# A long one-core attention, MLP and expert kernel: three pieces of the first batch are written at other places of its order

## The chip, the cores and the metric

The kernel runs on 1 core of a Trainium2 chip. Its time is the device time of one execution in microseconds (us); lower is better. Two times stand side by side below: the time of a run, and the span of one profiled execution, from its first to its last instruction. Engines are named as in the profile: PE is TensorE (matmul; PEld its weight loads), DVE is VectorE, ACT is ScalarE, POOL is GpSimd, SP is SyncE, which issues nearly all DMAs here.

## The reference: what is computed

The sizes are small enough to state: 4 batches, 12 heads, 448 positions, head dimension 64; a hard-swish MLP of 768 to 2048 to 768 on the 1792 tokens; then 8 experts of 768 to 1024 to 768, 224 tokens each.

```python
q_n, k_n = rmsnorm(q, g_q), rmsnorm(k, g_k)            # over the head dimension
scores = q_n @ k_n.T / 8
attn = exp(scores - max(scores)); attn /= sum(attn) + 1e-9
x = (attn @ v).transpose(0, 2, 1, 3).reshape(1792, 768)

h = x @ w_in                                           # w_in, w_out arrive in 64 bits
g = h * clip(h + 3, 0, 6) / 6
x2 = g @ w_out

logits = x2 @ w_gate          # greedy: the highest logits first, 224 tokens for each expert
out[tokens of e] = relu(x2[tokens of e] @ w1[e]) @ w2[e]
```

## The kernel before

**Tiling.** Attention works on pairs of heads: pair i (numbered from 0 in the code and in this text) holds two heads of one batch, so a batch is 6 pairs and there are 24. The first MLP matmul of batch b runs while the pairs of batch b+1 are worked on. A float32 product is split in a high and a low part (kh and kl, xh and xl, the two halves of w) and summed from three matmuls.

**The order is written out by hand.** In the part that the change touches, nothing is scheduled by a tool: every piece of work is put on a list with a number, its time in steps (`at(t, fn, ...)`), the list is sorted by that number, and each of the five engines then runs its own instructions in exactly that order. A pair starts every 16 steps. The steps are no clock, only places in the order; engines wait for one another by semaphores, and an instruction that waits holds all that stands behind it on its engine. SP is such a queue too: a DMA whose data is not there yet holds the DMAs behind it.

**What a pair needs, by name.** `squares` (ACT, L251) squares q and k of a pair; `fold` (POOL, L256) and `sums` (DVE, L267) add them up; `guess` (DVE, L271 and L272) makes a first inverse root and `invert` (POOL, L279 to L282, three rounds) refines it: the Newton steps. From pair 4 on two pairs share these small tiles and go through `guess` and `invert` together. `norm` (POOL, L298) scales q and k to `xn`; `transp` transposes them on PE (L315) and makes qh and kh on ACT (L324) and ql and kl on DVE (L327). `s1` makes scores on PE (L338) and their maxima mx on DVE (L341); `mt` transposes the maxima (PE L347) and lays them out as mr (DVE L349). `sT` makes the scores the other way round (PE L360) and ACT takes the exponent to ph (L371). `pv` multiplies by v (PE L449, copied out by ACT L452 to xn_t), `padd` and `psums` add the exponents up (POOL L442, PE L460 or L465, copied to rb by ACT L467).

**The trip of the sums.** The row sums leave for DRAM and come back in another shape: sum_dr (SP L471), rs (L476), reciprocal rr on DVE (L482, L483), rec_dr (L487), rb (L493, two DMAs). Then POOL multiplies (`xmul`, L497), ACT makes xh (L507) and POOL the low part xl (L505). The numbers `TX0` are the steps of these eight pieces for the pairs of the first batch.

**Narrowing.** w_in arrives in 64 bits. `conv` makes 32 bits of it in 16 units: a load of 768 KB (wraw, SP L159, 14 steps ahead), four steps (ACT L141, DVE L142, L143, L144, one step apart), and a store to DRAM (SP L174, one step behind the last). Two wraw buffers and two result buffers rotate. Unit u stands at `T_CI + D_CI * u`. From step 98 on the MLP of batch 0 loads the narrowed weights back (win_v, L181) and splits them (L118, L119).

PSUM is one pool of 8 banks that all matmuls take in turn, so a late reader of one bank can hold a later matmul.

Of the kernel before, what the change touches and what calls it, by code (L numbers as in the profile page):

```python
# [21 lines left out]
def kernel(  # L22
# [48 lines left out]
    T_SUMS, T_INV, T_INV0, NG0 = -50, -42, -35.5, 10  # L71
# [4 lines left out]
    T_ADD, T_PV, T_SUM = (6, 13), (15.6, 15.62, 15.64, 15.66), 15.7  # L76
    T_RS, T_RL, T_REC, T_RO, T_RB, T_X, T_XH, T_XL = 19.5, 21.5, 24, 25.5, 28, 33, 35.5, 39.5
    GD, WD2, C_ST = 12, 8, 5
    TX0 = (20, 23, 27, 29, 32.5, 39, 42, 46)
    QMAJOR = (NP - 1, B * NP - 1)  # L80
    T_CI, D_CI, T_CO, D_CO, T_CL = 20, 10, 180, 12, 14


    order = ExitStack()
# [652 lines left out]
    def at(t, fn, *args):  # L737
        events.append((t, len(events), fn, args))
# [7 lines left out]
    for i in range(NH // 2):  # L746
        t = 16 * i
        at(t + T_LOAD, load, i)
        at(t + T_VLOAD, vload, i)
        g = GROUP[i]  # L750
        first = 16 * g[0]
        t_sq = first + T_SUMS + 4 * (i - g[0])
        at(t_sq, squares, i)
        if 2 <= i < NG0:
            at(t_sq + 2, fold, i)
            t_sq += 3
        at(t_sq, sums, i)
        late_g = 4 <= g[0] < NG0
        if i == g[-1]:
            at(t_sq if 2 <= i < NG0 else first + T_INV, guess, g)  # L760
            at(first + (T_INV0 if late_g else T_INV), invert, g)
        at(t + (T_INV0 + 0.1 if late_g and i == g[0] else T_NORM), norm, i)
        at(t + T_Q, transp, i, 0)
        at(t + T_K, transp, i, 1)
        at(t + T_V, vsplit, i)
        for c in range(NCH):
            at(t + (T_S1[c] if i else -24 + 0.1 * c), s1, i, c)
            at(t + (T_ST[c] if i else (-9, -8.9, 1, 1.1)[c]), sT, i, c)
            if i in QMAJOR:
                for s in range(2):  # L770
                    at(t + T_AV[s][c], av, i, s, c)
            else:
                at(t + T_PV[c], pv, i, c)
        at(t + (T_MT if i else -21), mt, i)
        if i in QMAJOR:
            at(t + T_NUM, normalize, i)
            at(t + T_XT, xt, i)
        else:
            for n in range(2 if i >= NP else 0):
                at(t + T_ADD[n], padd, i, n)  # L780
            at(t + T_SUM, psums, i)
            tx = TX0 if i < NP else (T_RS, T_RL, T_REC, T_RO, T_RB, T_X, T_XH, T_XL)
            for d, fn in zip(tx, (rs_out, rs_in, rec, r_out, r_in, xmul)):
                at(t + d, fn, i)
            at(t + tx[6], xsplit, i, False)
            at(t + tx[7], xsplit, i, True)
        if (i + 1) % NP == 0:
            at(t + T_MLP[i // NP], mlp_next, i // NP)
# [1 line left out]
    at(8 * H + 2, prefetch, 0)  # L790
    at(8 * H + 14, prefetch)
    for u in range(NF if wide else 0):
        for out_, t in ((0, T_CI + D_CI * u), (1, T_CO + D_CO * u)):
            at(t - T_CL, conv, (out_, u), -1)
            for part in (0, 1, 2, 3, C_ST):
                at(t + part, conv, (out_, u), part)
# [446 lines left out]
    for pi, (t, hfs) in enumerate(passes):  # L1243
# [10 lines left out]
        for f in range(NF):  # L1254
            i, k = divmod(f, QF)
# [139 lines left out]
```

## Time and profile before

| | us |
|---|---|
| runs (3) | 1159.02, 1164.75, 1165.14; median 1164.75 |
| time of the profiled execution | 1162.06 |
| its span | 1160.2 |
| PE busy in it | 1099.2 (95%) |
| DVE, ACT, POOL busy | 692.2, 521.3, 464.6 |

The span is 1.9 us shorter than the time of the same execution, the part outside the first and last instruction. PE is busy nearly throughout from about 130 us on; its gaps lie in the first batch. A timeline row tells start, length, engine, line, operation and shapes, and in brackets how long the engine stood idle before it and what ended that. A row of the windows tells a stretch, its length, the busy time of each engine with its instruction count, the granted clock of TensorE as a share of full speed (1.00 is 2.4 GHz, 0.50 is 1.2 GHz, and values between are mixtures of the two), and the busy share and rate of the DMA engines.

### The profile page before, as it was taken

To read this page: it belongs to the slowest core of one execution; us is meant where nothing else is said; L and a number is where in the kernel's file an instruction comes from. 1 tells how busy PE (TensorE), PEld (TensorE's weight loads), DVE (VectorE), ACT (ScalarE), POOL (GpSimd) and SP (SyncE) were. 2 spreads that over 40 slices of the span, in tenths; PEclk is the share of its full clock that TensorE was granted. 3 is DMA by queue.
4 is the path that set the end of the run, shared out by engine and by line. 5 is a ranking of instruction groups with operands and counts; after the bars stand their busy time and mean duration, and the time that the engine had idled before them with its cause. 6 is when DMAs were issued, how large, how long until landed. Compare 5 with 4: busy or idle time off the path is not lost.

```text
span 1160.2 us, 19232 instructions
## 1 busy us (share of the span) xinstructions
PE 1099.2 (95%) x7073; PEld 880.7 (76%) x7073; DVE 692.2 (60%) x1440; ACT 521.3 (45%) x941; POOL 464.6 (40%) x410
## 2 busy tenths in 40 slices
PE   4978899999999999999999999999997999999997
PEld 3446556766766667787767888888887899999997
DVE  7877877886677845212341666666665846555550
ACT  4655555745545556533542111111114766666551
POOL 4665555664445533112444000000004677775540
PEclk9987989999999999999999999999998999999999
DMA  4575998978777887659996222222237888877731
GB/s 133 145 197 148 248 300 252 309 238 297 251 250 253 257 288 239 222 190 276 356 310 204 78 69 82 64 76 71 70 104 185 245 262 247 248 227 217 226 130 39
DMA packets 215357, 232.17 MB, mean 200 GB/s; under 512 B 28296, under 2 KB 188384, under 8 KB 215264
## 3 DMA queue, kind: packets, MB, share of 16 engines
q1 hardware_dynamic: 211936, 219.94, 61.6%
q0 software_dynamic: 3328, 11.01, 3.1%
q8 instruction: 55, 0.90, 0.3%
q14 instruction: 38, 0.31, 0.1%
HBM read 179.82 MB, written 51.09 MB: 199 GB/s over the span
## 4 chain that ended last, share of the span: by engine, by line
PE 67%; DVE 10%; DMA 9%; issue 5%; POOL 4%; ACT 3%; SPq 1%; POOLq 0%; DVEq 0%; ACTq 0%
PE y L1195 19%; PE h L559 15%; PE y L1347 8%; PE h L1283 5%; PE st L360 4%; PE av L449 4%; PE h L1285 3%; DMA w_hl<-w 2%; DMA we_s<-in_moe_w_dram 2%; DVE mx L341 2%; PE rt L988 1%; PE lg L601 1%; PE sm L465 1%; DMA gr<-g_dr 1%; DVE cv L143 1%
## 5 line engine op out<-in xcount | busy, mean ns | idle before, releaser
L559 PE MATMUL h<-xh,w 128*128 128x448 f32 x768 | 239.9, 382 | 1.0 <-DVE mx L341 0.5
L559 PEld LDWEIGHTS h<-xh,w 128*128 128x128 f32 x768 | 143.3, 191 | 35.9 <-issue 22.1
L559 PE MATMUL h<-xl,w 128*128 128x448 f32 x384 | 145.7, 379 | 0.0
L341 DVE TENSOR_REDUCE mx<-s 112x1 f32<-112x448 f32 x192 | 105.9, 611 | 51.6 <-PE s L338 51.3
L1133 ACT ACTIVATE g2h<-gr 128x512 fp32r<-128x512 f32 x60 | 37.9, 631 | 206.1 <-PE y L1195 161.6
L1195 PE MATMUL y<-woh,g2l 128*128 128x512 f32 (+1 forms) x448 | 124.8, 344 | 1.0 <-POOL g2l L1098 1.0
L1195 PE MATMUL y<-woh,g2h 128*128 128x512 f32 (+1 forms) x448 | 125.3, 345 | 0.0
L1195 PE MATMUL y<-wol,g2h 128*128 128x512 f32 (+1 forms) x448 | 125.2, 344 | 0.0
L1098 POOL TENSOR_TENSOR g2l<-gr,g2h 128x512 fp32r<-128x512 f32 x14 | 19.0, 1361 | 240.6 <-DMA gr<-g_dr 209.0
L119 POOL TENSOR_TENSOR wel<-we_s,weh 128x768 fp32r<-128x768 f32 x48 | 96.3, 2010 | 45.4 <-ACT weh L118 37.0
L118 ACT ACTIVATE weh<-we_s 128x768 fp32r<-128x768 f32 x107 | 88.4, 841 | 57.9 <-DMA we_s<-in_moe_w_dram 39.3
L119 DVE TENSOR_TENSOR wel<-we_s,weh 128x768 fp32r<-128x768 f32 x59 | 78.3, 1334 | 60.3 <-ACT weh L118 53.6
L371 ACT ACTIVATE ph<-st 112x448 f32<-112x448 f32 x192 | 93.0, 545 | 40.8 <-PE st L360 39.7
L442 POOL TENSOR_TENSOR pa<-ph 112x448 f32<-112x448 f32 x68 | 85.6, 1279 | 44.2 <-ACT ph L371 44.2
L1283 PE MATMUL h<-xe,weh 128*128 128x448 f32 x318 | 100.4, 375 | 2.0 <-DVE xe L1234 2.0
L559 PEld LDWEIGHTS h<-xl,w 128*128 128x128 f32 x384 | 73.2, 191 | 11.9 <-issue 7.0
L1195 PEld LDWEIGHTS y<-woh,g2l 128*128 128x128 f32 x448 | 72.0, 189 | 10.7 <-POOL g2l L1098 1.3
L1195 PEld LDWEIGHTS y<-woh,g2h 128*128 128x128 f32 x448 | 71.9, 189 | 10.6 <-issue 1.5
L1195 PEld LDWEIGHTS y<-wol,g2h 128*128 128x128 f32 x448 | 71.9, 189 | 9.1 <-issue 0.7
L1285 PE MATMUL h<-xe,wel 128*128 128x224 f32 x318 | 76.6, 268 | 0.0
L562 ACT ACTIVATE r<-h,half 128x448 f32<-128x448 f32 x64 | 40.6, 634 | 77.7 <-PE h L559 67.3
L497 POOL TENSOR_TENSOR xn_t<-xn_t,rb 128x448 f32<-128x448 f32 x22 | 25.8, 1175 | 119.7 <-DMA rb<-rec_dr 119.7
(252 smaller groups left out, 2386.1 us busy)
## 6 DMA issues: line engine op xcount, KB each, us to landing
we_s<-in_moe_w_dram SPq DMA_DIRECT2D x128, 384.0 KB
w<-w_hl SPq DMA_DIRECT2D x32, 768.0 KB
gr<-g_dr SPq DMA_DIRECT2D x52, 256.0 KB
wraw<-in_moe_w_in_dram SPq DMA_DIRECT2D x16, 768.0 KB
win_v<-w SPq DMA_DIRECT2D x32, 384.0 KB
w_hl<-w SPq DMA_DIRECT2D x16, 768.0 KB
wraw<-in_moe_w_out_dram SPq DMA_DIRECT2D x16, 768.0 KB
g_dr<-g SPq DMA_DIRECT2D x48, 224.0 KB
```

What stands on the lines that cost most here:

```text
L118: nc.scalar.activation(hi, raw, AF.Copy)
L119: eng.tensor_tensor(lo, raw, hi.bitcast(F32), op=OP.subtract)
L341: mx = nc.vector.tensor_reduce(MX[i][:, s, c:c + 1], pp[s][:CP, :S], axis=AX.X, op=OP.max)
L360: nc.tensor.matmul(pp[s][:CP, :S], a[r], b[r], start=(n == 0), stop=(n == len(todo) - 1))
L371: nc.scalar.activation(e, pp[s][:CP, :S], AF.Exp)
L442: nc.gpsimd.tensor_tensor(PA[i, s, n], PP[i, s, 2 * n][0], PP[i, s, 2 * n + 1][0], op=OP.add)
L449: nc.tensor.matmul(p[r, :S], vvs[i % 2][:, s, c, V0:V0 + 64], PP[i, s, c][0], start=(c == 0), stop=(c == NCH - 1))
L559: nc.tensor.matmul(p[:, :S], lhs[:, c], x[:, c], start=(n == 0), stop=(n == 3 * NC - 1))
L1195: nc.tensor.matmul(pp[hf][:, :COLS[hf].stop - COLS[hf].start], a[:, f % QF], w[:, COLS[hf]], start=(f == 0 and n == 0), stop=(f == NF - 1 ...
L1283: mm = [lambda: nc.tensor.matmul(p[:, :4 * CP], wh[:, fo], x.rearrange("d k t -> d (k t)"), start=(c == 0), stop=(c == NC - 1), skip_group ...
L1285: lambda: nc.tensor.matmul(p[:, :2 * CP], wl[:, fo], x[:, 0], start=False, stop=False, skip_group_check=True)]
L1347: nc.tensor.matmul(p[:CP, :HW], a[:, f, tk], w[:, o], start=(f == 0 and n == 0), stop=(f == FB - 1 and n == 2))
```

## The change

Three things move; no instruction is added or removed.

- For the pair groups (4, 5), (6, 7) and (8, 9) the second pair's squares, with its fold and sums, stand 2.1 steps later (6.1 instead of 4 steps behind the first). These second pairs are 5, 7 and 9 counted from 0.
- The narrowing units of w_in get a list of steps of their own: units 0 and 8 go 4.3 steps later, 3 and 11 go 6.3 later, 5 and 13 go 2.3 later, 6 and 14 go 1.7 earlier; the others stay. Loads and stores of a unit move with it.
- The low part xl of a first-batch pair stands at step 44.4 instead of 46.

```diff
-    TX0 = (20, 23, 27, 29, 32.5, 39, 42, 46)
+    TX0 = (20, 23, 27, 29, 32.5, 39, 42, 44.4)
...
-    T_CI, D_CI, T_CO, D_CO, T_CL = 20, 10, 180, 12, 14
+    T_CO, D_CO, T_CL = 180, 12, 14
+    T_CI = (24.3, 30, 40, 56.3, 60, 72.3, 78.3, 90, 104.3, 110, 120, 136.3, 140, 152.3, 158.3, 170)
...
-        t_sq = first + T_SUMS + 4 * (i - g[0])
+        late_g = 4 <= g[0] < NG0
+        t_sq = first + T_SUMS + (6.1 if late_g else 4) * (i - g[0])
...
-        for out_, t in ((0, T_CI + D_CI * u), (1, T_CO + D_CO * u)):
+        for out_, t in ((0, T_CI[u]), (1, T_CO + D_CO * u)):
```

PE's order is the same before and after. The new code is one line longer, so lines from 82 on count one higher in the rows of the change.

**The second squares and the narrowing of unit 3, on ACT.** These are ACT's instructions from pair 5's qh on; sq are the squares of pair 7, cv is the narrowing. Before:

```order
L324 ACTIVATE qh<-t,gq_72 128x448
L251 ACTIVATE sq<-ld_q 112x512
L251 ACTIVATE sq<-ld_k 112x512
L141 ACTIVATE cv<-wraw 128x768
L324 ACTIVATE kh<-t,gk 128x448
L304 ACTIVATE vv_134<-ld_v 112x8x64
L371 ACTIVATE ph<-st 112x448 x4
```

The same stretch in the changed kernel:

```order
L325 ACTIVATE qh<-t,gq_72 128x448
L325 ACTIVATE kh<-t,gk 128x448
L252 ACTIVATE sq<-ld_q 112x512
L252 ACTIVATE sq<-ld_k 112x512
L305 ACTIVATE vv_134<-ld_v 112x8x64
L372 ACTIVATE ph<-st 112x448 x4
L142 ACTIVATE cv<-wraw 128x768
```

kh moved ahead of three instructions; the narrowing step went behind the four exponents.

**The same place on DVE.** ql, kl and mr are the operands that PE waits for, st_2 the sums of the pair's squares, mx the maxima. Before:

```order
L327 SCALAR_TENSOR_TENSOR ql<-t,gq_72,qh 128x448
L142 TENSOR_SCALAR cv<-cv 128x768
L327 SCALAR_TENSOR_TENSOR kl<-t,gk,kh 128x448
L143 SCALAR_TENSOR_TENSOR cv<-wraw,cv 128x768
L267 TENSOR_REDUCE st_2_883<-sq 112x8 x2
L271 TENSOR_SCALAR st_2_883<-st_2_883 112x32
L272 TENSOR_SCALAR st_2_884<-st_2_883 112x32
L144 SCALAR_TENSOR_TENSOR cv<-wraw,cv 128x768
L349 TENSOR_TENSOR mr<-t,place 128x448
L341 TENSOR_REDUCE mx_130<-s_948 112x1
```

In the changed kernel:

```order
L328 SCALAR_TENSOR_TENSOR ql<-t,gq_72,qh 128x448
L328 SCALAR_TENSOR_TENSOR kl<-t,gk,kh 128x448
L350 TENSOR_TENSOR mr<-t,place 128x448
L268 TENSOR_REDUCE st_2_883<-sq 112x8 x2
L272 TENSOR_SCALAR st_2_883<-st_2_883 112x32
L273 TENSOR_SCALAR st_2_884<-st_2_883 112x32
L342 TENSOR_REDUCE mx_130<-s_942 112x1
L342 TENSOR_REDUCE mx_130<-s_943 112x1
L342 TENSOR_REDUCE mx_130<-s_966 112x1
L342 TENSOR_REDUCE mx_130<-s_967 112x1
L143 TENSOR_SCALAR cv<-cv 128x768
L144 SCALAR_TENSOR_TENSOR cv<-wraw,cv 128x768
```

kl and mr follow ql directly, and the narrowing steps (cv) went behind the four maxima, so ahead of rr.

**The trip of pair 4's sums on SP.** These are SP's DMAs from the sums' store on; w_97<-cv is the store of a narrowed unit, wraw the load of one. Before:

```order
L471 DMA sum_dr_1261<-rb 4x448
L236 DMA ld_v<-in_v_dram 112x2x256
L174 DMA w_97<-cv 128x6x128
L159 DMA wraw<-in_moe_w_in_dram 128x6x256
L476 DMA rs<-sum_dr_1261 112x2x8
L229 DMA ld_q<-in_q_dram 112x2x256
L229 DMA ld_k<-in_k_dram 112x2x256
L487 DMA rec_dr_1359<-rr 112x8
```

In the changed kernel:

```order
L472 DMA sum_dr_1258<-rb 4x448
L237 DMA ld_v<-in_v_dram 112x2x256
L477 DMA rs<-sum_dr_1258 112x2x8
L230 DMA ld_q<-in_q_dram 112x2x256
L230 DMA ld_k<-in_k_dram 112x2x256
L160 DMA wraw<-in_moe_w_in_dram 128x6x256
L488 DMA rec_dr_1360<-rr 112x8
```

The store and the load of a narrowing unit no longer stand between sum_dr and rs. On POOL the xl of pairs 1 and 3 moved from behind Newton steps and two xn ahead of those Newton steps, and the xl of pair 4 ahead of two pa.

## Rows read from the trace of the kernel before

**Rows 1.** Windows by stage: stretch, length, engines' busy time, clock, DMA share, GB/s.

```profile
38.00:65.00 27.00, 22.88 (x166) 11.94 (x166) 23.87 (x43) 17.93 (x35) 14.97 (x22) 1.00 0.58 156
65.00:83.00 18.00, 13.77 (x81) 6.62 (x77) 12.16 (x24) 8.50 (x17) 11.60 (x19) 0.81 0.71 198
96.00:116.00 20.00, 16.81 (x97) 13.86 (x95) 15.63 (x25) 9.18 (x17) 11.78 (x20) 0.70 0.49 130
130.00:170.00 40.00, 36.55 (x204) 26.91 (x205) 32.67 (x55) 21.95 (x40) 20.23 (x15) 0.90 0.88 262
400.00:1160.00 760.00, 739.44 (x4948) 641.72 (x4948) 387.72 (x892) 299.89 (x539) 252.97 (x172) 0.99 0.59 182
```

**Rows 2.** Timeline of PE: rows with a wait in front of them.

```profile
39.56 0.46 PE L338 MATMUL s<-kh,qh 64*112 64x448 f32 x2 [0.72 <-ACT kh L324]
...
51.19 0.32 PE L347 MATMUL t<-ident,mx 112*128 112x112 f32 x1 [1.28 <-DVE mx L341]
...
64.42 0.32 PE L347 MATMUL t<-ident,mx 112*128 112x112 f32 x1 [1.69 <-DVE mx L341]
...
67.23 0.71 PE L338 MATMUL s<-kh,qh 64*112 64x448 f32 x2 [1.50 <-ACT kh L324]
...
81.00 0.97 PE L338 MATMUL s<-kh,qh 64*112 64x448 f32 x2 [2.59 <-ACT xn_t L452]
...
97.58 0.46 PE L338 MATMUL s<-kh,qh 64*112 64x448 f32 x2 [1.00 <-ACT kh L324]
...
102.36 0.46 PE L360 MATMUL st<-mr,minus 64*112 64x448 f32 x2 [1.33 <-DVE mr L349]
...
162.82 0.71 PE L360 MATMUL st<-qh,kh 64*112 64x448 f32 x1 [2.68 <-DVE g L564]
```

**Rows 3.** Timeline of PE: the same 16 matmuls twice, and three marks without wait.

```profile
53.84 3.23 PE L449 MATMUL av<-ph,vv 112*64 112x448 f32 x16
...
69.75 5.01 PE L449 MATMUL av<-ph,vv 112*64 112x448 f32 x16
...
82.90 0.26 PE L347 MATMUL t<-ident,mx 112*128 112x112 f32 x1
...
115.43 0.39 PE L347 MATMUL t<-ident,mx 112*128 112x112 f32 x1
...
129.79 0.71 PE L360 MATMUL st<-qh,kh 64*112 64x448 f32 x2
```

**Rows 4.** Timeline of ACT ahead of pair 5's kh.

```profile
65.78 0.88 ACT L141 ACTIVATE cv<-wraw 128x768 f32<-128x768 f32 x1
66.56 0.62 ACT L324 ACTIVATE kh<-t,gk 128x448 fp32r<-128x448 f32 x1
```

**Rows 5.** Timeline of POOL and ACT around pair 1's low part.

```profile
69.93 1.77 POOL L497 TENSOR_TENSOR xn_t<-xn_t,rb 128x448 f32<-128x448 f32 x1 [3.10 <-DMA rb<-rec_dr]
...
71.74 0.58 ACT L507 ACTIVATE xh<-xn_t 128x448 fp32r<-128x448 f32 x1 [1.28 <-POOL xn_t L497]
...
79.25 1.13 POOL L505 TENSOR_TENSOR xl<-xn_t,xh 128x448 fp32r<-128x448 f32 x1
...
80.41 0.54 ACT L452 ACTIVATE xn_t<-av 128x448 f32<-128x448 f32 x1 [7.31 <-POOL xl L505]
```

**Rows 6.** The chain that ended last: start, length, what.

```profile
46.63 4.51 DMA rec_dr<-rr
...
64.23 5.57 DMA rb<-rec_dr
...
100.61 7.88 DMA rs<-sum_dr
```

**Rows 7.** Timeline of DVE: pair 4's row sums.

```profile
108.59 0.28 DVE L482 TENSOR_TENSOR rr<-rs 112x8 f32<-112x8 f32 x1 [4.16 <-DMA rs<-sum_dr]
```

**Rows 8.** Tile wraw, 30 to 130 us: one narrowing step, lengths in ns (min/median/max).

```profile
L143 DVE SCALAR_TENSOR_TENSOR cv<-wraw,cv x9: 947/962/2680, 41.8 to 117.1; 128x768 int32<-128x768 int32 x9
```

**Rows 9.** Timeline of POOL: pair 4's multiplication.

```profile
121.77 1.13 POOL L497 TENSOR_TENSOR xn_t<-xn_t,rb 128x448 f32<-128x448 f32 x1 [10.43 <-DMA rb<-rec_dr]
```

More of the change, by code (lines that the diff above doesn't have):

```diff
@@ L757 @@
         at(t_sq, sums, i)
-        late_g = 4 <= g[0] < NG0
         if i == g[-1]:
```

## The prediction

> **What bounds the kernel now.** I read the windows first. From 400 us on PE is busy 739 of 760 us at a clock of 0.99 [rows 1]: nothing in the change touches that part, and a microsecond won ahead of it stays won, because PE runs the same instructions in the same order and has no slack in which a late start could be caught up. So the question is only how much earlier PE comes out of the first batch. There the picture differs from window to window. From 38 to 65 us the clock is full and DVE is busy 23.87 of 27 us, PE 22.88: both are close to their limit. From 65 to 83 us, from 96 to 116 us and from 130 to 170 us no engine is that full, and the clock is granted at 0.81, 0.70 and 0.90 [rows 1], which means that for a part of these stretches TensorE ran at 1.2 instead of 2.4 GHz. What this costs is seen in a pair of rows: the same sixteen matmuls took 3.23 us at full clock and 5.01 us in a stretch with the lower one [rows 3]. Over a stretch the loss is its length times what the clock lacks: 18 x 0.19 = 3.4 us, 20 x 0.30 = 6.0 us, 40 x 0.10 = 4.0 us.
>
> Then I went down PE's timeline for the waits. Eight of them carry the argument [rows 2]: three for kh (0.72, 1.50 and 1.00), two for the last maxima (1.28 and 1.69), one for the copy xn_t on ACT (2.59), one for mr (1.33) and one at 162.82 for the MLP's g on DVE (2.68). Each of the three stretches with a lowered clock has one or several of these waits at its start or shortly before it.
>
> Last the engines behind those waits. ACT made the kh of pair 5 at 66.56, directly behind a narrowing step that began at 65.78 [rows 4], and in the order the two squares stand ahead of that. ACT's xn_t copy at 80.41 had stood idle 7.31 us for POOL's xl [rows 5], and POOL did that xl at 79.25, behind the Newton steps and both xn. DVE stood 4.16 us before rr [rows 7], for an rs that was 7.88 us under way [rows 6].
>
> **The change part by part.** I give for each stretch what could come back at most, and what I take.
>
> *38 to 65 us.* kh of pair 3 follows qh directly, so the wait of 0.72 goes. Ahead of the four maxima one long narrowing step (0.96 us, the median of L143 [rows 8]) goes behind them, so the maxima and the matmul that waits for them (1.28, later 1.69) come earlier. But DVE has only 3.1 us of slack in these 27 and its work stays the same, so what moves behind these maxima stands ahead of the next ones. At most 0.72 + 1.28 + 1.69 = 3.7 us come back, at least 0.7; I take 0.7 + half of 2.97 = **2.2 us**, which puts the mark at 64.42 at about 62.2.
>
> *65 to 83 us.* The 1.50 us wait for kh goes, as ACT no longer has squares and narrowing in front of it. The 2.59 us wait for xn_t goes too, since xl is done before the Newton steps. With the PE gaps gone the clock may stay up: 3.4 us. Together 7.5 us at most. Something else becomes late, though: the Newton steps now wait for xh and xl. Counted from the end of xn_t (69.93 + 1.77 = 71.70), the Newton steps and two xn took until 79.25, where xl began: 7.5 us [rows 5]. With xh (0.58) and xl (1.13) in front all this ends 1.7 us later, counted from the landing of rb, and PE needs those xn for the transposes ahead of its mark at 82.90 [rows 3]. So the wait for xn_t is in part replaced by one for xn. I take half of 7.5 less 1.7 = **2.0 us**; bounds: a loss of 1.7 and a gain of 7.5.
>
> *83 to 116 us.* kh (1.00) and mr (1.33) are no longer late: kl and mr follow ql on DVE with no narrowing between. With the clock's 6.0 us that is 8.3 us at most. Also rs now leaves ahead of the unit's store and its 768 KB load, not behind them; if it then takes about the 4.51 us of the rec_dr in [rows 6], which had such a load in front of it, DVE's 4.16 us wait shrinks by 3.4 us. That wait has narrowing and the maxima for the mark at 115.43 behind it, so it is what makes the rest usable and is not counted a second time. Against it stands the second xl ahead of Newton steps, 1.7 us. Half of 8.3 less 1.7 gives **2.4 us**; bounds: a loss of 1.7 and a gain of 8.3. The mark at 115.43 would then be near 109.
>
> *116 to 130 us.* Here the change costs. Unit 8's narrowing moves behind the last maxima, so one long step (0.96) more stands ahead of the reciprocal of pair 5, and POOL does an xl (1.13) before the two pa that PE waits for: **2.1 us** later, nothing if the earlier rb gives POOL its room, 3.0 us if both long steps count.
>
> *130 to 170 us.* Unit 11's narrowing leaves the place between ql, kl and g. The wait of 2.68 goes, and the lowered clock behind it (4.0 us) may: 6.7 us at most. But the DMA engines are busy 0.88 of this stretch [rows 1], and the split weights come when they land. I take half, **3.3 us**; bounds 0 and 6.7.
>
> The later units 5, 6, 13 and 14 I cost at nothing: what hides them is the distance in the order, since each unit's store still stands several loads ahead of the one that reads it back. If that cover were gone, the MLP would wait for unit 13 by its 2.3 steps, about 2.3 us (the 32 steps of two pairs take from 82.90 to 115.43 [rows 3], 1.0 us a step).
>
> Sum: 2.2 + 2.0 + 2.4 - 2.1 + 3.3 = 7.8 us. The profiled execution took 1162.06 us (span 1160.2); this gives 1154.3. The profiled execution lies 2.7 us under the median of the runs, and the four times together have a mean of 1162.7, so I name **1155 us**.
>
> A rule of the Trainium skill speaks against the new places of the narrowing. L143 takes 0.96 us as a rule, and 2.68 us in the longest of nine cases [rows 8]. The Trainium skill, page "SBUF — State Buffer", section "Who interferes with whom", says that DVE and GpSimd share a pair of ports as an exclusive lock: a DVE instruction with two inputs in SBUF contends with a GpSimd instruction that reads SBUF, and the one that comes second is blocked. By that rule the maxima, which come from PSUM, never suffer, and every narrowing step that is moved beside POOL's Newton steps can; the trace has such a long case, but the row alone doesn't show what stood in its way. The second rival below is worked out from the row, without the rule.
>
> **The rivals.**
>
> *All of it comes back.* If the clock stays up in all three stretches and no new wait comes, the halves that I took become wholes: 3.7 + 5.8 + 6.6 - 2.1 + 6.7 = 20.7 us. For it speaks that waits stand before each lowered stretch; against it that POOL's line to xn remains the last thing in two of them. Half-way between, at 14 us, the time is 1148.
>
> *The narrowing meets POOL.* Six units move late, with two long steps each. Three of these twelve that take 2.68 instead of 0.96 us on DVE's path to the maxima cost 5.2 us; 2.6 us of the gain remain: 1160 us. For it speaks the row itself [rows 8]; against it that the median of the nine is 0.96.
>
> *Slower: POOL's line gets later.* Newton now waits for xl, xl for xh and xn_t, and these for rb. In SP's new order the load of unit 6 stands ahead of pair 2's rb. rb took 5.57 us with a load in front [rows 6]; another 768 KB at the 198 GB/s of that stretch [rows 1] is 3.9 us. If POOL's line is then 1.7 + 3.9 = 5.6 us later at both places where PE ends up waiting for xn, the second and third terms turn from +4.4 to -11.2 us, and with the other three (+3.4) the kernel is 7.8 us slower: 1170 to 1171 us. It decides from the point at which POOL's line is 3.9 us later at both places than I have it (7.8 / 2). For it: POOL already stood idle for rb by 3.10 and 10.43 us [rows 5, 9]. Against it: rs gets rid of two DMAs in front of it, which is earlier in the same trip.
>
> The trace shows what a load in front does to a small DMA: rec_dr carries 896 numbers and took 4.51 us [rows 6]. The Trainium skill, page "DMA: Bandwidth & Descriptors", section "Queues, rings and completion order", says that each DMA engine takes the descriptors of one ring in their order. By that rule a load placed ahead of rb is paid in full, and one taken from ahead of rs is won in full; the row agrees.
>
> **How the numbers follow.** My forecast, a gain of 4 to 12 us (1151 to 1159), gets 0.50; the full return 0.14; the narrowing or another cover that eats the gain to within 0.5% 0.25; slower 0.11. A difference of 0.5%, 5.8 us, is about what a measurement of this kernel can tell from none. Faster by more than that: the first two cases, 0.64. Same 0.25, slower 0.11. The range leaves out the slower case and about the upper half of the full return: 1146 to 1164 us.
>
> **What would show it.** In the trace after, the three kh waits are gone and kh begins as qh ends; the mark of 64.42 comes near 62, that of 82.90 near 78 to 79, that of 115.43 near 109, the row at 129.79 near 125, and the wait at 162.82 is gone. Clock shares of 0.81 and 0.70 rise. The forecast is wrong if PE's new waits for xn (from POOL) are as long as the old ones, if the clock is as low as before, or if rb lands no earlier after 80 us.

## Result and the profile after

The changed kernel took 1170.14 us (median of 8 runs, 1165.78 to 1174.41), the kernel before 1163.10 us in the same series (8 runs, 1159.02 to 1165.14). The ratio is 1.0065, 95% interval 1.0047 to 1.0083: 0.65% or some 7 us slower, where the prediction said 1155 us and gave slower a chance of 0.11. The profiled execution took 1171.55 us, its span is 1169.8 us.

These are the windows of the changed kernel for the stretches of [rows 1]; the columns are the same.

```profile
38.00:65.00 27.00, 23.38 (x158) 12.98 (x159) 23.04 (x41) 17.50 (x34) 18.62 (x22) 0.87 0.54 150
65.00:83.00 18.00, 12.04 (x84) 6.39 (x82) 15.41 (x27) 9.82 (x20) 11.41 (x18) 0.88 0.75 202
96.00:116.00 20.00, 12.84 (x79) 10.10 (x78) 13.79 (x27) 8.64 (x17) 12.62 (x20) 0.75 0.84 241
130.00:170.00 40.00, 34.54 (x193) 23.46 (x193) 29.70 (x49) 21.30 (x39) 22.88 (x18) 0.91 0.83 248
400.00:1160.00 760.00, 745.73 (x4984) 646.49 (x4983) 397.16 (x910) 305.63 (x550) 256.86 (x175) 0.99 0.61 185
```

The stretches with a lowered clock (0.81, 0.70, 0.90 before) rose to 0.88, 0.75 and 0.91, as forecast; but the first one fell from 1.00 to 0.87, and it also fell in the two stretches that the rows leave out: from 0.87 to 0.78 at 83 to 96 us, and from 0.87 to 0.75 at 116 to 130 us. POOL, busy 14.97 us of the first stretch before, is now busy 18.62 us with as many instructions (x22). PE's timeline says what it waits for now: start, length, matmul, and in brackets the wait in front of it.

```profile
50.33 0.60 PE L316 MATMUL t<-ident,xn 112*128 112x112 f32 x4 [2.33 <-POOL xn L299]
52.04 1.01 PE L316 MATMUL t<-ident,xn 112*128 112x112 f32 x4 [1.11 <-POOL xn L299]
...
65.98 0.32 PE L348 MATMUL t<-ident,mx 112*128 112x112 f32 x1 [0.38 <-DVE mx L342]
...
82.03 2.01 PE L316 MATMUL t<-ident,xn 112*128 112x112 f32 x8 [5.52 <-POOL xn L299]
...
83.83 0.39 PE L348 MATMUL t<-ident,mx 112*128 112x112 f32 x1
...
106.45 3.25 PE L401 MATMUL av<-vv,ph 112*112 112x66 f32 x16 [1.76 <-ACT ph L372]
...
112.96 1.01 PE L316 MATMUL t<-ident,xn 112*128 112x112 f32 x4 [3.25 <-POOL xn L299]
...
120.33 0.39 PE L348 MATMUL t<-ident,mx 112*128 112x112 f32 x1
...
135.21 0.71 PE L361 MATMUL st<-qh,kh 64*112 64x448 f32 x2
...
169.52 0.45 PE L339 MATMUL s<-kh,qh 64*112 64x448 f32 x2 [2.56 <-DVE mr L350]
```

Set beside [rows 2]: the three waits for kh, the one for xn_t and the one for g are gone, those for the maxima have shrunk from 1.28 and 1.69 to below 0.4. In their place stand four waits for xn, which POOL makes: 2.33 + 1.11 + 5.52 + 3.25 = 12.2 us. The wait for mr at 102.36 is gone, and one of 2.56 us for another mr came at 169.52. Taking all gaps on PE between the same two matmuls, which lie at 40.05 and 260.05 us in the kernel before, PE stood idle 20.8 us of 220.0 there and 27.3 us of 228.3 after: 6.4 of the 8.3 us are waits; the rest goes with a lower clock (0.89 against 0.91 over these stretches). Behind 275 us the two kernels run in step, 7.9 us apart at 275 and 7.5 at 840 us; at the end it is 9.5.

What the waits near 50 us did to the clock stands in two windows of the changed kernel:

```profile
51.50:58.00 6.50, 5.96 (x29) 4.03 (x31) 3.78 (x7) 4.10 (x9) 2.59 (x4) 0.50 0.56 156
58.20:66.00 7.80, 7.42 (x59) 3.62 (x55) 7.22 (x11) 4.89 (x11) 5.60 (x4) 1.00 0.80 217
```

Behind the two waits for xn, 6.5 us ran at 0.50, that is at 1.2 GHz; in the kernel before the clock is 1.00 from 38 to 65 us. Between the matmuls at 40.05 and 64.42 (before) the waits sum to 3.40 us before and 3.82 after, while the stretch got 1.9 us longer: 0.4 us of that are waits, and 1.5 us go with the lower clock.

Why xn is late stands on POOL's timeline at the first of these waits.

```profile
43.02 0.24 POOL L280 TENSOR_TENSOR st<-st 112x32 f32<-112x32 f32 x1
43.34 1.01 POOL L281 TENSOR_TENSOR st<-st,st 112x32 f32<-112x32 f32 x1
44.44 0.87 POOL L282 TENSOR_SCALAR st<-st 112x32 f32<-112x32 f32 x1
45.39 1.10 POOL L283 TENSOR_TENSOR st<-st,st 112x32 f32<-112x32 f32 x1
...
47.73 1.42 POOL L283 TENSOR_TENSOR st<-st,st 112x32 f32<-112x32 f32 x1
49.23 1.04 POOL L299 TENSOR_TENSOR xn<-ld_q,st 112x512 f32<-112x512 f32 x1
```

The same time on DVE:

```profile
41.56 2.21 DVE L342 TENSOR_REDUCE mx<-s 112x1 f32<-112x448 f32 x4
43.69 0.55 DVE L143 TENSOR_SCALAR cv<-cv 128x768 int32<-128x768 int32 x1
44.27 0.96 DVE L144 SCALAR_TENSOR_TENSOR cv<-wraw,cv 128x768 int32<-128x768 int32 x1
...
45.47 0.91 DVE L145 SCALAR_TENSOR_TENSOR cv<-wraw,cv 128x768 int32<-128x768 int32 x1
...
48.09 0.95 DVE L144 SCALAR_TENSOR_TENSOR cv<-wraw,cv 128x768 int32<-128x768 int32 x1
```

A Newton step on POOL takes 0.24 us beside the maxima, and 0.87 to 1.42 us beside one of the two long narrowing steps (L144, L145), which itself keeps its 0.91 to 0.96 us: it is POOL that pays, with about the length of the step beside it. The twelve Newton steps of a pair group take 3.8 us undisturbed. From the first step's start to the last one's end, the groups of pairs (4, 5), (6, 7) and (8, 9) took 5.75, 5.50 and 3.78 us in the kernel before and 7.42, 5.99 and 5.42 us in the changed one. A trip of sums is later as well; its rows stand under the experiments.

### The profile page after: what moved, and what is told of

The parts are those of the page before. It is cut to its first block, busy times and chain, and to the rows that moved or that the text cites. A ratio compares the mean times of both kernels' runs of the same rounds, so it can differ in the third digit from the quotient of the medians.

```text
span 1169.8 us, 19220 instructions
## 1 busy us (share of the span) xinstructions
PE 1102.7 (94%) x7073; PEld 885.5 (76%) x7073; DVE 694.0 (59%) x1440; ACT 521.7 (45%) x941; POOL 470.7 (40%) x410
## 4 chain that ended last, share of the span: by engine, by line
PE 69%; DMA 9%; DVE 7%; issue 5%; POOL 4%; ACT 3%; SPq 1%; POOLq 0%; ACTq 0%; DVEq 0%
PE y L1196 19%; PE h L560 15%; PE y L1348 8%; PE h L1284 5%; PE st L361 5%; PE av L450 4%; PE h L1286 3%; DMA we_s<-in_moe_w_dram 2%; DMA w_hl<-w 1%; PE sm L466 1%; PE t L316 1%; PE rt L989 1%; DMA rec_dr<-rr 1%; PE lg L602 1%; DMA gr<-g_dr 1%
## 5 line engine op out<-in xcount | busy, mean ns | idle before, releaser
L119 ACT ACTIVATE weh<-we_s 128x768 fp32r<-128x768 f32 x107 | 88.3, 840 | 61.5 <-DMA we_s<-in_moe_w_dram 42.4
L1196 PEld LDWEIGHTS y<-woh,g2h 128*128 128x128 f32 x448 | 72.3, 190 | 10.9 <-issue 1.5
L1196 PEld LDWEIGHTS y<-woh,g2l 128*128 128x128 f32 x448 | 72.3, 189 | 10.8 <-POOL g2l L1099 1.3
```

Of the source, the lines that this page charges most:

```text
L119: nc.scalar.activation(hi, raw, AF.Copy)
L1196: nc.tensor.matmul(pp[hf][:, :COLS[hf].stop - COLS[hf].start], a[:, f % QF], w[:, COLS[hf]], start=(f == 0 and n == 0), stop=(f == NF - 1 ...
```

## Experiments

**The theories.** *A:* the moved narrowing steps lie beside POOL's Newton steps (and xl in front of them), so xn and with it PE are late. *B:* SP's new order of loads and stores makes the trip of the sums later. *C:* any displacement changes where the clock falls, and the loss is chance. After the second series a further rival to A came up, *D:* DVE's line is close to its limit all through the first batch, so a narrowing step costs about the same wherever it stands. Each ratio is to the kernel before, run in the same series, with its 95% interval. Several kernels leave steps of the narrowing out; their expectations say which.

**e1, the squares alone.**

```diff
-        t_sq = first + T_SUMS + 4 * (i - g[0])
+        t_sq = first + T_SUMS + (6.1 if late_g else 4) * (i - g[0])
```

> Only the second squares of the pairs 5, 7 and 9 behind kh; narrowing and xl as before. Theory A (the changed kernel lost its time on POOL's line: narrowing on DVE fell on the Newton steps and xl stands ahead of them, so PE waits for xn and its clock falls): this part touches neither, the kh waits of 0.72, 1.50 and 1.00 us go, 1 to 4 us faster than before. Theory B (the loads and stores of the narrowing, moved on SP, make the trip of the sums later): also unharmed, 1 to 4 us faster. Theory C (any shift of this stretch moves the lowered clock to another place, and the sign is chance): anything from 5 us faster to 7 us slower.

1162.15 us, 0.9998 (0.9979 to 1.0018). PE was 3.5 us ahead at 76 to 82 us, since the kh waits were gone, and had given it back by 86 us to the waits for xn_t (2.06) and xn (1.00). So this part is worth nothing by itself, where A and B had both expected 1 to 4 us. It does touch POOL's line: with the later squares, unit 0's narrowing (at its old place) stands ahead of their sums on DVE, the first Newton group begins at 44.45 instead of 41.38 us, and PE waits 0.65 + 1.11 us for xn near 50 us though the group takes only 4.18 us.

**e2, the narrowing list alone.**

```diff
-        for out_, t in ((0, T_CI + D_CI * u), (1, T_CO + D_CO * u)):
+        for out_, t in ((0, T_CI[u]), (1, T_CO + D_CO * u)):
```

> Only the narrowing's new list of steps. Theory A: pair 4's Newton steps take 7 us or more instead of 5.7, PE waits 2 us or more for xn near 50 us; 2 to 5 us slower than before. Theory B: all of the loss sits here, 7 us slower. Theory C: no order between the parts.

1168.36 us, 1.0052 (1.0029 to 1.0075): nearly the whole loss. PE's wait for xn near 50 us came (1.99 + 0.92 us), but the first Newton group took 6.16 us, not 7 or more: the 7.42 us need the later squares as well. The time, some 6 us over the kernel before, lies between A's 2 to 5 and B's 7. Without the early xl, POOL's slow Newton steps (7.38 us for pairs (6, 7)) stand in front of xl, and PE waits at the same place for what hangs on it, as this row of PE's timeline shows:

```profile
82.97 1.24 PE L339 MATMUL s<-kh,qh 64*112 64x448 f32 x2 [7.11 <-ACT xn_t L453]
```

**e3, the early xl alone.**

```diff
-    TX0 = (20, 23, 27, 29, 32.5, 39, 42, 46)
+    TX0 = (20, 23, 27, 29, 32.5, 39, 42, 44.4)
```

> Only xl ahead of the Newton steps. Theory A: PE waits for the xn of pairs 6 and 8, 1 to 4 us slower than before. Theory B: within 1 us of before. Theory C: no order between the parts.

1163.99 us, 1.0010 (0.9991 to 1.0030): no difference that can be told. One of the waits that A expected is there, 2.56 us for xn at 79.92, but it stands in the place of one for xn_t that was as long (2.59).

**e4, the change without the early xl** (the line of e3 the other way round in the changed kernel).

> The changed kernel with xl back behind the Newton steps. Theory A: 2 to 5 us faster than the changed kernel, so 2 to 5 us slower than before; the 5.5 us wait for xn near 82 us falls under 4 us. Theory B: as slow as the changed kernel, 7 us over before.

1167.54 us, 1.0044 (1.0025 to 1.0063). Against the changed kernel's 1.0065 the early xl may cost 2 us; the intervals overlap, so this isn't settled. A's time came; its wait didn't: near 82 us PE stands 8.13 us for xn_t, which hangs on xl, instead of 5.52 us for xn. The parts (0.0, +0.5 and +0.1%) add up to about the whole, and the list brings the loss in each kernel that has it. That speaks against C.

**e5 and e6, five units left out beside the Newton steps, and five away from them.** Both are the changed kernel.

```diff
         if part < 4:
-            steps[part]()
+            if part == 0 or out_ or n not in (0, 1, 3, 4, 7):
+                steps[part]()
```

In e6 the numbers are (2, 5, 6, 8, 9). The line keeps ACT's step (part 0) in both, so only the three DVE steps of a unit are left out, not ACT's as the first expectation has it (and that of e12, further down).

> The changed kernel, but units 0, 1, 3, 4 and 7 go without their narrowing (one step on ACT, three on DVE each; these parts of w_in are stored without having been made, so the kernel leaves out a part of the computation). All other places of the order stay, SP's included. These are the units whose DVE steps ran beside POOL's Newton steps in the changed kernel. Theory A (a POOL instruction gets longer beside a narrowing step on DVE): the three groups of Newton steps go from 7.42, 5.99 and 5.42 back to about 3.8 us each, the waits for xn near 50 (3.4 together), 82 (5.5) and 113 (3.3) lose more than half, and the time falls by 6 to 12 us, to 1158 to 1164. Theory B (SP's order makes the trip of the sums later): the waits near 82 and 113 stay, since SP's order stays; the time falls by 0 to 3 us, 1167 to 1170.

> The control for the one before: the changed kernel, but units 2, 5, 6, 8 and 9, whose DVE steps ran away from the Newton steps, go without their narrowing (as many steps left out on each engine). Theory A: the Newton groups stay at about 7.4, 6.0 and 5.4 us; what is won is DVE's time alone (unit 5's steps stand ahead of pair 3's rr, 2 us), 0 to 4 us, 1166 to 1170. Theory B: since DVE's steps make no difference by themselves, this kernel and the one before come out alike, within 2 us.

e5: 1162.37 us, 0.9998 (0.9979 to 1.0018). e6: 1160.84 us, 0.9989 (0.9973 to 1.0006). On POOL it went as A says: the Newton groups took 3.82, 3.77 and 3.77 us in e5 and 7.43, 6.91 and 5.38 in e6. A's time for e5 held too; of its waits the one near 82 us fell only to 3.30 us. On PE, e5 was 8.6 us ahead of the changed kernel at its mark of 83.83 and e6 2.0 us. But from there to 175 us e5 won 2.0 us more and e6 10.5, and in the end e6 came out no slower. My control was none for the whole time: A's expectation for it (1166 and more) failed, B's (both alike within 2 us) held in the time while its waits didn't. This is where D came from.

Besides, e5 lost 5.5 us of its lead between the matmuls that lie at 203 and 211 us in the kernel before. First its window there, then the row of ACT that holds the exponents back, then PE's wait.

```profile
200.00:230.00 30.00, 25.80 (x145) 18.48 (x143) 18.58 (x27) 17.60 (x32) 16.33 (x13) 0.89 0.97 317
```

```profile
206.23 0.84 ACT L119 ACTIVATE w<-win_v 128x768 fp32r<-128x768 f32 x1 [4.26 <-DMA w_hl<-w]
```

```profile
208.08 0.71 PE L340 MATMUL s<-kh,qh 64*112 64x448 f32 x1 [3.14 <-ACT ph L373]
```

The DMA engines are busy 0.97 of this stretch, and ACT waits until the split weights of the MLP have been stored, with the exponents queued behind it. Who comes early waits here.

**e7, SP's loads back at their old places in the changed kernel.**

```diff
-            at(t - T_CL, conv, (out_, u), -1)
+            at(6 + 10 * u if not out_ and u in (0, 3, 6, 8, 11, 14) else t - T_CL, conv, (out_, u), -1)
```

> The changed kernel, but SP's 768 KB loads of units 0, 3, 6, 8, 11 and 14 stand at the places they had before; the steps and the stores stay at the new places. Theory B: the trip of pair 2's and pair 3's sums gets back the time it lost (rb of pair 3 issued at 96 rather than 100 us), the waits for xn near 82 and 113 lose about half, 1164 to 1167. Theory A: the Newton groups keep their length, the waits stay, and the time stays within 2 us of the changed kernel's, 1168 to 1172.

1171.67 us, 1.0084 (1.0053 to 1.0114). The waits for xn at 81 and 112 us are 5.52 and 4.63 us. B falls, as far as these six loads go: the loads of units 5 and 13 and all stores stay at their new places, and unit 7's load, of which more below, stands at its old step in both kernels.

What a load in front does to a small DMA is seen here: in e7 rs leaves SP at 103.71, behind unit 8's load, and rr can start 4.6 us later; in the changed kernel it leaves at 104.33 with no unit's load between sum_dr and it, and rr starts 1.8 us later. The load in front costs 2.8 us here, less than the 3.9 that the prediction's slower case took for one. These are DVE's rows, first of the changed kernel, then of e7:

```profile
106.11 0.31 DVE L483 TENSOR_TENSOR rr<-rs 112x8 f32<-112x8 f32 x1 [1.94 <-DMA rs<-sum_dr]
```

```profile
108.31 0.17 DVE L483 TENSOR_TENSOR rr<-rs 112x8 f32<-112x8 f32 x1 [4.95 <-DMA rs<-sum_dr]
```

rr is 2.2 us later in e7; of that only 0.4 is left when rb leaves (111.80 and 112.22).

**e8, the late units and the squares only.**

```diff
-    T_CO, D_CO, T_CL = 180, 12, 14
-    T_CI = (24.3, 30, 40, 56.3, 60, 72.3, 78.3, 90, 104.3, 110, 120, 136.3, 140, 152.3, 158.3, 170)
+    T_CO, D_CO, T_CL = 180, 12, 14
+    T_CI = (20, 30, 40, 50, 60, 70, 80, 90, 100, 110, 120, 136.3, 140, 152.3, 158.3, 170)
```

The early xl is taken back too.

> The kernel before, with the second squares moved as in the change and of the narrowing list only the late units (11 and 13 later, 14 earlier); units 0 to 10 and xl as before. Theory A: nothing is lost up to 130 us, since no step moves beside the Newton steps of the first batch's groups; the wait of 2.68 us at 162.8 goes, and half of it or all stays won: 1159 to 1161. A rival (C): the late part of the list costs as well, through mr or a lower clock behind 170 us: 1163 to 1167.

1165.24 us, 1.0026 (1.0009 to 1.0043): A's expectation failed, the rival's range held. At the place of the g wait PE is 3.5 us ahead of the kernel before; at the next mr all of it is gone into a wait of 3.69 us. These are DVE's rows there.

```profile
162.55 0.96 DVE L120 TENSOR_TENSOR w<-win_v,w 128x768 fp32r<-128x768 f32 x1 [3.27 <-ACT w L119]
163.43 0.62 DVE L350 TENSOR_TENSOR mr<-t,place 128x448 fp32r<-128x448 f32 x1
```

In the kernel before the same two stand at 162.69 and 163.56, with no wait. So DVE is freed of the narrowing and then waits for ACT's half of the MLP's split weights, and ACT for a DMA: 3.06 us at 161.62, where the trace names the load of v; in the changed kernel the same row of ACT (L119) at 167.04 stood 3.09 us for the store w_hl. The split weights come no earlier, and mr is queued behind them. This part of the list gains nothing that lasts. Beside e1 (0.9998) it may cost some 3 us, though the intervals overlap; in the profiled execution PE is 0.4 us behind the kernel before at 275 us and 3.4 at the end, and what happens in between wasn't followed up.

**e9 and e10, units 0 and 3, or unit 5, back at their old steps** in the changed kernel: 24.3 and 56.3 become 20 and 50, or 72.3 becomes 70.

> The changed kernel with units 0 and 3 alone at the steps they had before (20 and 50). Theory A (the narrowing beside the Newton steps): the Newton groups of pairs (4, 5) and (6, 7) go from 7.42 and 5.99 to about 5.7 and 5.5 us, PE is 2 to 4 us earlier at 56 and 82 us than in the changed kernel, and kl and mr wait for narrowing again; the third group and pair 3's sums stay late, so of the loss of 7 us about 2 to 4 come back: 1166 to 1168. The rival, that the loss comes from unit 5 ahead of pair 3's reciprocal alone: 1169 to 1171.

> The changed kernel with unit 5 alone at its step of before (70), so that its narrowing no longer stands between pair 3's sums and their reciprocal on DVE. If that trip is a second cause: the reciprocal of pair 3 ends about 2 us earlier, rb of pair 3 is issued at 96 to 98 instead of 99.9 us, the third Newton group starts earlier and PE is 2 to 4 us earlier at 109 us: 1166 to 1168. If the Newton steps beside unit 7 alone make that loss: no change, 1169 to 1171.

e9: 1169.14 us, 1.0057 (1.0038 to 1.0077). e10: 1168.16 us, 1.0051 (1.0030 to 1.0071). In time neither can be told from the changed kernel, and A's 1166 to 1168 for e9 failed. On PE, e9 is no earlier at the mark of 65.98 (0.6 us later) though its first Newton group took 4.18 us: it began at 44.34 instead of 41.73, for unit 0 now stands ahead of the first inverse root on DVE. That speaks for D. e10 did what was expected up to 115 us: 2.7 us earlier at the mark of 120.33. The rows behind that are DVE's, first of the kernel before, then of the changed one (with POOL's xl beside it), and SP's of the changed kernel:

```profile
89.11 0.94 DVE L144 SCALAR_TENSOR_TENSOR cv<-wraw,cv 128x768 int32<-128x768 int32 x1
89.97 0.69 DVE L482 TENSOR_TENSOR rr<-rs 112x8 f32<-112x8 f32 x1
```

```profile
90.23 1.15 POOL L506 TENSOR_TENSOR xl<-xn_t,xh 128x448 fp32r<-128x448 f32 x1 [0.95 <-ACT xh L508]
90.31 1.88 DVE L144 SCALAR_TENSOR_TENSOR cv<-wraw,cv 128x768 int32<-128x768 int32 x1
92.11 0.69 DVE L483 TENSOR_TENSOR rr<-rs 112x8 f32<-112x8 f32 x1
...
92.95 1.32 DVE L145 SCALAR_TENSOR_TENSOR cv<-wraw,cv 128x768 int32<-128x768 int32 x1
```

```profile
94.34 0.39 SPq L160 DMA_DIRECT2D wraw<-in_moe_w_in_dram  x1
94.78 0.53 SPq L488 DMA_DIRECT2D rec_dr<-rr  x1
...
99.88 1.22 SPq L494 DMA_DIRECT2D rb<-rec_dr  x2
```

In the kernel before, unit 5's three steps stood ahead of pair 3's rr too, but in between the maxima, from 85.63 on. Here the first comes only at 89.72, behind them, and rr begins at 92.11. Unit 7's load, next on SP, needs unit 5's buffer, so it leaves when L145 ends (94.27), and rec_dr waits behind it. In the kernel before rec_dr left at 91.14 and rb at 96.08; here it is 94.78 and 99.88, and with the early xl the Newton steps of pairs (8, 9) began at 106.36 instead of 101.86. In e10 rr began at 90.93, 1.2 us earlier than here, and rec_dr left at 92.10, 2.7 us earlier; rb left at 97.10.

**e11, all narrowing clear of the Newton steps up to unit 7.** The list is in the expectation; xl as before.

> A version built on the theory: the squares as in the change, xl as before, and the narrowing list written so that up to unit 7 no step stands behind the first inverse root of a pair group (where the Newton steps run) or ahead of a reciprocal of the sums; most units start 0.1 step behind kl. The list is 36.1, 43.1, 51.9, 68.1, 75.1, 83.9, 100.1, 107.1, 116.1, 123.1, 132.1, 139.1, 147.5, 154.5, 162, 170, each load 12 steps ahead instead of 14. Theory A: all three Newton groups at about 3.8 us, PE ahead of the kernel before by 3 to 8 us at 82 to 116 us; what is left at the end depends on the DMA-bound part near 205 us: 1154 to 1161. A rival (the places don't matter, only how much is narrowed): 1161 to 1166. Another: the tighter spacing behind unit 6 makes SP late, 1166 and more.

1179.33 us, 1.0148 (1.0124 to 1.0173), the slowest of all: A's time failed, and that of the last rival (1166 and more) held. The Newton groups took 3.82, 3.83 and 3.82 us and PE was 4.9 us ahead of the kernel before at 82 us; at 104 us it was 0.4 behind, at 211 us 12.7. Its longest wait, on PE's timeline:

```profile
209.08 0.71 PE L361 MATMUL st<-qh,kh 64*112 64x448 f32 x1 [5.40 <-ACT xn_t L453]
```

ACT stood 7.11 us for the same store of split weights as in e5 ahead of that. Sixteen units that start 16 steps later and must end at the same step come mostly 7 to 9 steps apart instead of 10.

**e12, ten units left out** (the edit of e5 with n > 9).

> The changed kernel with the narrowing steps of units 0 to 9 all left out on ACT and DVE (these parts of w_in are stored without having been made, so the kernel leaves out a part of the computation; loads and stores stay). The two kernels that leave out five units each were 10.4 and 11.5 us ahead of the changed kernel near 180 us. If what is won early stays won, as the prediction took it, this kernel is 18 to 22 us ahead there and at the end: 1148 to 1152. If the stretch near 205 us, with the DMA engines at 0.97, sets a floor: still 15 us or more ahead at 180, but no more than 10 behind 260: 1159 to 1162.

1151.43 us, 0.9906 (0.9882 to 0.9930). It was 17.2 us ahead of the changed kernel at 170 us, 18.2 at 275 us and 17 at the end. Its time is what the first of the two readings gave. Near 205 us, between the same two matmuls that cost e5 5.5 us of its lead, it lost 1.9 us; that is no fixed wall.

**e13 and e14, three units beside the Newton steps or apart from them.** Both leave out the DVE steps of seven units and have the same loads; e14 differs in

```diff
             at(t - (8 if not out_ and u in (2, 6, 9) else T_CL), conv, (out_, u), -1)
+            if not out_:
+                t = {0: 36.1, 4: 68.1, 7: 100.1}.get(u, t)
```

> Of units 0 to 9 only 0, 4 and 7 are narrowed on DVE, at the steps of the changed kernel (24.3, 60 and 90), which lie beside the Newton steps; the others go without their three DVE steps (these parts of w_in are stored without having been made, so the kernel leaves out a part of the computation). Units 2, 6 and 9, which are among those left out, load 8 steps ahead and stand at 49, 80 and 112. DVE has room in this kernel, so what is measured is the meeting with POOL. Theory A: the three Newton groups take 5.4 to 6.5 us each, the transposes wait for xn after each of them, and PE is 3 to 6 us later at 109 us than in the next kernel. The rival (what costs is that DVE has the work at all, not where): PE within 1 us of the next kernel there.

> The same as the one before, with the same work left out and the same loads, but the narrowing of units 0, 4 and 7 and their stores stand at 36.1, 68.1 and 100.1, behind the kl of the next pair, where no Newton step runs. Theory A: all Newton groups at 3.8 us, as with the ten left out (PE near 8 us ahead of the kernel before at 109 us), and the time lies 2 to 5 us under that of the kernel before this one. The rival: the same time within 1.5 us, since the same DVE work is done.

e13: 1160.11 us, 0.9984 (0.9966 to 1.0002). e14: 1157.72 us, 0.9955 (0.9936 to 0.9974). The Newton groups took 6.06, 5.51 and 5.52 us in e13 and 3.82, 3.79 and 3.77 in e14. The waits for xn in e13,

```profile
49.02 0.60 PE L317 MATMUL t<-ident,xn 112*128 112x112 f32 x4 [0.95 <-POOL xn L300]
...
77.14 2.01 PE L317 MATMUL t<-ident,xn 112*128 112x112 f32 x8 [5.04 <-POOL xn L300]
...
104.73 1.01 PE L317 MATMUL t<-ident,xn 112*128 112x112 f32 x4 [4.10 <-POOL xn L300]
```

and in e14:

```profile
74.38 0.60 PE L317 MATMUL t<-ident,xn 112*128 112x112 f32 x4 [3.30 <-POOL xn L300]
...
102.19 1.01 PE L317 MATMUL t<-ident,xn 112*128 112x112 f32 x4 [3.84 <-POOL xn L300]
```

PE is 2.5 us earlier in e14 at the mark of 115.43 and 3.0 at 170 (both as the kernel before counts), the time 2.4 us shorter. The means of the two sets of 12 runs differ by 2.7 us, with a 95% interval of about 0.6 to 4.8. This is the meeting at equal work on DVE (ACT's step and the store of the three units move with it): 5.7 us more on POOL in three groups, of which 2.5 reach PE, and the waits for xn shown are 2.95 us longer in sum. The rival (within 1 us on PE) falls where DVE has room to spare; A holds in the time, and PE's 2.5 lie just under the 3 to 6 us expected. In the two profiled executions (1158.24 and 1158.81 us) the lead doesn't last: e14 loses 4.1 us of it from 300 to 400 us, where nothing was moved, so the time rests on the runs and not on the trace.

**e15 and e16, the first five units clear, all others as before,** with the squares moved (e15) and not (e16).

```diff
+    T_CI = (12.1, 32.2, 40.2, 48.3, 64.3, 70, 80, 90, 100, 110, 120, 130, 140, 150, 160, 170)
```

> A version for both kernels to be beaten by: the squares as in the change, xl and the units from 5 on as before, and units 0, 1, 2, 3 and 4 at 12.1, 32.2, 40.2, 48.3 and 64.3, so that no narrowing stands beside the first two Newton groups (4, 5) and (6, 7) and unit 0 falls into DVE's idle 2.01 us at 33 to 35 us. Theory A with the measured price (three groups with 5.7 us of lengthening cost PE 2.6 us): the lengthening of before in these two groups (5.75 and 5.50 instead of 3.8, 3.6 us together) goes, PE is 2 to 4 us ahead at 82 us, and 1 to 3 us are left at the end: 1159 to 1161. The rival (DVE's line is the bound wherever the narrowing stands, and what is won is given back by the 86th us, as with the squares alone): 1161 to 1164.

> The same with the squares where the kernel before has them. Theory A: the Newton groups at 3.8 us as well, the kh waits of up to 1.5 us of before stay: within 1 us of the version with the squares moved, 1159 to 1162. The rival: 1161 to 1164.

e15: 1165.34 us, 1.0038 (1.0023 to 1.0053). e16: 1164.41 us, 1.0033 (1.0008 to 1.0057). The Newton groups were at 3.8 us as planned, and nothing was won: in e15 PE waits 2.21 us for the maxima at 65 us, 3.00 us for ACT's xn_t at 80 us and 2.29 us for ph at 108 us. A's expectation failed, and both times lie a little above the rival's range too. With all units narrowed, D describes the kernels better: a step that is taken from beside POOL stands in front of something that PE also needs. But with e8 and e11 these are four other orders that lost 0.3 to 1.5% without longer Newton steps, so C isn't excluded. No version that computes everything beat the kernel before.

## Why the prediction was wrong

The prediction's terms against the marks of both traces (before [rows 2, 3], after the fences above; minus is a gain; rounding makes the rows 0.1 us more than the sum):

| stretch | forecast | measured |
|---|---|---|
| to 64.42 | -2.2 | +1.6 |
| to 82.90 | -2.0 | -0.6 |
| to 115.43 | -2.4 | +4.0 |
| to 129.79 | +2.1 | +0.5 |
| to 170 | -3.3 | -0.7 |
| behind, to 275 | 0 | +3.2 |
| sum | -7.8 | +7.9 |

*What bounds it.* That PE's early waits set the end and that behind the first batch the kernels run in step holds for the changed kernel: 7.9 us at 275 us stand against 7 us in the runs. That a microsecond won early stays won is wrong in part: e1 gave back 3.5 us within 10 us, e8 3.5 us at the next mr, e5 5.5 us near 205, e14 4.1 us between 300 and 400.

*38 to 65 us* has the wrong sign, and this is the step that failed first. The term moved a narrowing step behind the maxima and asked what it delays on DVE. It didn't ask what runs on POOL at that moment, though the text knew the Newton steps to stand there. The waits for the maxima did shrink (2.97 to 0.4 us), but POOL's Newton steps grew from 5.75 to 7.42 us and PE stood 3.4 us for xn. In sum the waits came out nearly equal (3.8 us against 3.4 from 40 us on); the clock, which the term left at 1.00, then fell to 0.50 for 6.5 us behind the waits for xn, and that is the larger part of the loss.

*65 to 83 us* took the Newton steps at their old length, and that xn would replace "in part" the wait for xn_t. It replaced it by more: 5.52 for 2.59 us. The gain of 2.8 us at 76 us was there; 3.0 were lost by 82 us.

*83 to 116 us* is the largest miss, 6.4 us. I took rs to be earlier and the rest with it. The trip of rs did get shorter, even by more than forecast (7.88 us before, rr 1.8 us behind it after), but I never looked at pair 3's trip: unit 5, which I costed at nothing, now comes late and directly ahead of that rr and holds rec_dr back behind unit 7's load; e10 gives 2.7 us of it back. The cover that I named for the later units, the distance from store to read-back, was the wrong cover: the first thing that waits for unit 5 is pair 3's rr on DVE.

*116 to 130 us* was costed too high by 1.6 us, for pair 4's rb did come earlier: its xn_t began at 116.52 instead of 121.77 [rows 9]. *130 to 170 us:* the g wait went, as said, but the split weights of the MLP took its place and held mr (2.56 us; 3.69 in e8). I had read the DMA engines' 0.88 as a reason to take half; the row to look at was the store that ACT waits for, which gives nothing earlier. *Behind 170 us* I put nothing; PE's waits there grew by 1.0 us (1.24 us for kl at 257.52 and 1.06 for mr at 260.18, against one of 1.04 for kl before), and the clock was 0.91 at 230 to 270 us against 0.96, which is 40 x 0.05 = 2.0 us at most.

*The rivals.* The slower case had the right line (POOL's, to xn, at the places near 82 and 113 us) and came within a microsecond of the time, 1170 to 1171 us. That the number fits is luck, for its price was put together wrongly: 1.7 us for xl and 3.9 us for a load in front of rb. e3 and e7 show little of either in the time; what made POOL late were the longer Newton steps, which the other rival had as a cost of DVE (2.68 us three times), and rr. The two rivals were one, and its chance should have been larger.

How much of the 7.9 us each cause has can't be said in full. The list carries about 0.5 of 0.65% (e2), of which its late units may be up to half (e8), with no Newton step of the first three groups beside them. Within it, unit 5 ahead of rr is 2 to 3 us on PE (e10). In place of three groups lengthened by 5.7 us (2.5 us on PE in e13), the change lengthens them by 1.67 + 0.49 + 1.64 = 3.8 us; at the same rate that is some 1.7 us, an estimate. The rest, the lower clock near 260 us among it, was not separated.

## What to carry to other kernels

When a step is moved on an engine's queue, list what runs on the other engines at its new place and what stands behind it in its own queue; the wait that it leaves is a gain only if the new place has no one who waits, and if what PE needs next (here the MLP's split weights, held by a store) comes earlier too. On an engine that is busy nearly nine tenths of a stretch such a place may not be found: both lists tried here that keep clear of the meeting (e11; e15 and e16) lost as well. A control that leaves out as much work elsewhere isn't one as long as that work costs there too; the same work at two places is.

## What the runs showed of the hardware

In the profiles of the two kernels and of the first twelve experiments, 98 Newton steps between 38 and 120 us ran beside no work of DVE and took 0.241 us on average; 259 ran beside the maxima and took 0.240 (longest 0.256); 41 ran beside one of the two long narrowing steps, alone or with the maxima, and took 0.87 to 1.43 us. The maxima have 112x448 elements from PSUM, the narrowing steps two inputs of 128x768 in SBUF. What I had not expected is who pays: a long narrowing step beside another long POOL instruction takes 1.88 us instead of 0.95 (at 90.31, with POOL's xl at 90.23), but beside the short Newton steps it is POOL that stands.

The Trainium skill, page "SBUF — State Buffer", section "Who interferes with whom", says that the shared ports are an exclusive lock, that the order of issue decides who blocks, and that a reduction never contends on this chip. The last agrees with these rows, 0.24 us beside the maxima. The lock agrees too: in 36 of the 41 cases the narrowing step had begun 0.12 to 0.17 us ahead of the Newton step, which then ended 0.1 us behind it. In the other five (1.42 and 1.43 us, as at 47.73 beside the step at 48.09) POOL had begun 0.36 us earlier by the profile and ended behind DVE's step all the same; by these starts the order doesn't explain them. The prediction named the rule, and priced it on the wrong engine.
